# Windowed attention before two feed-forward parts: first blocks of 128 columns, tables and sums in pieces, the general pass placed last

## Chip, cores and metric

The kernel runs on one core of a Trainium2 chip. The metric is the device time of one execution in microseconds; lower is better. All operands are float32.

## The reference, cut to what matters

```python
scores = q @ k.T / sqrt(D)                       # B=2, H=8, S=768, D=64
rel = pos[:, None] - pos[None, :]
keep = (pos[None, :] < n_global) | ((rel >= 0) & (rel < n_local))   # 8 and 96
scores = where(keep, scores - slope[h] * dist, -1e9)                # dist: |rel|, or n_local for global keys
x = softmax(scores) @ v                          # then (B*S, H*D) = (1536, 512)
...
for e in range(4):                               # gated part, F = 1024
    out += p[:, e:e+1] * (relu(x @ w1[e]) @ w2[e])
h = out @ w_in                                   # last part, F = 2048
y = (h * clip(h + 3, 0, 6) / 6) @ w_out
```

## The kernel before, in words

**Attention.** A *pair* is two heads on a chunk of 256 queries: 6 chunks (three for each of two batches) by 4 pairs of heads, 24 pairs. A pair has two blocks of 128 queries. Each block sees 256 columns of keys: 96 previous and 32 first ones, then its own 128. The first block of a batch has nothing before it, so its first 128 columns are masked by a table of its own. For every pair (`plan_pair`, L305) the steps are: load of q and k into one of four places of `qkraw` (L316) and of v (L323) on SP's queue; scores on PE (L344); bias by table, scale and minimum on DVE (L357); exponential and row sum on ACT (L371); reciprocal on DVE (L380, L381); normalisation on POOL (L389); transposes on PE (L402); copies out of PSUM on ACT for the first block and on DVE for the second (L414); products with v on PE (L426); copy of the result on ACT (L436). The tables (`plan_bias`, L271) are made on DVE for head 0 (L279 to L282, L285) and scaled on POOL for heads 1 to 7, twice seven instructions of 256 columns (L298).

**Feed-forward parts.** 48 steps of 256 hidden columns each. Every float32 operand is split into a high part (ACT cast, L230) and a low part (DVE subtraction, L235), and a product is three matmuls (L858, L862, L865 for the first layer, L1037, L1040, L1041 for the second). The first layer is computed by seven products with sums of blocks, in the manner of Strassen and Winograd: four sums of x (T1 to T4 in `plan_x`, L576; on POOL for batch 0, L614) and four sums of weights (S1 to S4 in `plan_weights`, L713; on POOL for the first two steps, L781 to L784, else on DVE). `finish` (L1066) copies a finished output out of PSUM, four blocks of 512 + 256 columns; the 256-column parts of two blocks share a bank. For the last part it issues the stores of the output (L1093).

**Order.** Nothing is ordered by hand. `Plan` (L53) holds pieces (engine, cost, emit, what they come after, rank) and lists them: whenever an engine is free in the plan's own time it takes the ready piece of lowest rank. The result is a fixed order for each engine. In gaps of PE's plan before the first feed-forward product, `keep_warm` (L240) puts matmuls on zeros.

**Two passes.** The device reads `n_global` and `n_local`, computes a flag (L160 to L167) and loads it into a register of every engine (L175). `body(True)` is the pass above, `body(False)` a general one for other sizes:

```python
    with tc.If(is_fast == 1) as cmp:
        body(True)
    with cmp.Else():
        body(False)
```

## Time and profile before

| | |
|---|---|
| median of 3 runs | 866.78 us (866.5 to 867.9) |
| the profiled execution | 867.49 us, its span 865.6 us |
| PE busy | 848.6 us (98%), granted clock 0.992 on the mean |
| DVE, ACT, POOL busy | 664.4, 406.1, 71.1 us |
| DMA | 148.14 MB, 171 GB/s on the mean |

The span runs from the first to the last instruction; the 1.9 us beside it are start and end of the execution. Busy time is time in which an engine has an instruction at work. Matmuls are pipelined, so a busy PE may still run at half its clock or wait inside; the stretches must be read one by one. POOL works only in the first 107 us.

### The profile page before, as it was taken

The page shows a single profiled execution, that of the slowest core. Times are in us where ns is not written, and L with a number is a line of the kernel's source. Part 1 is how long each engine was busy: PE and PEld are TensorE (multiplying, and loading weights), DVE is VectorE, ACT ScalarE, POOL GpSimd, SP SyncE. Part 2 cuts the span into 40 slices and gives each one's busy share as a digit, 9 for nine tenths or more (in the row PEclk, how much of TensorE's full clock was granted, in tenths as well). Part 3 has the DMA queues.
Part 4 walks back from the last instruction along what each step waited for, and adds up shares of the span by engine and source line. Part 5 has one row for each costly group of instructions (what it writes and reads, how often), then busy time and mean ns, then how long its engine had stood idle before and what let it go on. Part 6 is the DMA issues. An engine that isn't in the chain of part 4 may idle for free.

```text
span 865.6 us, 13712 instructions
## 1 busy us (share of the span) xinstructions
PE 848.6 (98%) x5117; PEld 770.7 (89%) x5117; DVE 664.4 (77%) x1362; ACT 406.1 (47%) x846; POOL 71.1 (8%) x127
## 2 busy tenths in 40 slices
PE   8998999999999999999999999999999999999996
PEld 6675799999999999999999999999999999999996
DVE  5889889898989988798786878878888774645442
ACT  5897853443434333443333333234655454545441
POOL 5478700000000000000000000000000000000000
PEclk9997999999999999999999999999999999999999
DMA  7663545455564666536656566556344353733402
GB/s 247 222 204 110 198 170 166 167 186 158 188 214 154 225 194 193 202 122 205 208 174 207 180 202 212 161 163 227 107 160 169 135 184 120 243 122 115 152 1 77
DMA packets 55833, 148.14 MB, mean 171 GB/s; under 512 B 6352, under 2 KB 6480, under 8 KB 55760
## 3 DMA queue, kind: packets, MB, share of 16 engines
q1 hardware_dynamic: 55472, 146.51, 51.6%
q8 instruction: 42, 0.69, 0.3%
q10 hardware_dynamic: 288, 0.69, 0.2%
q14 instruction: 31, 0.25, 0.1%
HBM read 110.45 MB, written 36.72 MB: 170 GB/s over the span
## 4 chain that ended last, share of the span: by engine, by line
PE 92%; DVE 3%; DMA 2%; ACT 1%; POOL 1%; issue 1%; DVEq 0%; SPq 0%; POOLq 0%
PE o L1040 15%; PE o L1041 15%; PE o L1037 15%; PE x_x L858 8%; PE x_x L865 8%; PE x_x L862 8%; PE w_w L862 6%; PE w_w L858 6%; PE w_w L865 6%; PE att_q L402 2%; PE att_q L426 2%; PE att_q L344 2%; DMA w<-qkraw 1%; DVE xol L235 1%; DMA wr<-in_w 1%
## 5 line engine op out<-in xcount | busy, mean ns | idle before, releaser
L1040 PE MATMUL o<-hh,w2l 128*128 128x512 f32 (+1 forms) x768 | 259.4, 338 | 0.0
L1041 PE MATMUL o<-hl,w2h 128*128 128x512 f32 (+1 forms) x768 | 258.9, 337 | 0.0
L1037 PE MATMUL o<-hh,w2h 128*128 128x512 f32 (+1 forms) x768 | 257.8, 336 | 0.0
L882 ACT COPY snap<-x_x 128x384 f32<-128x384 f32 x144 | 69.0, 479 | 199.2 <-PE x_x L865 199.2
L895 DVE TENSOR_TENSOR c_c<-w_w,snap 128x384 f32<-128x384 f32 x144 | 80.0, 555 | 105.1 <-ACT w2h L230 61.0
L1041 PEld LDWEIGHTS o<-hl,w2h 128*128 128x128 f32 x768 | 144.4, 188 | 16.0
L1037 PEld LDWEIGHTS o<-hh,w2h 128*128 128x128 f32 x768 | 144.4, 188 | 13.3
L1040 PEld LDWEIGHTS o<-hh,w2l 128*128 128x128 f32 x768 | 144.5, 188 | 12.6
L858 PE MATMUL x_x<-xoh,w1h 128*128 128x384 f32 x384 | 129.3, 337 | 0.0
L865 PE MATMUL x_x<-xoh,w1l 128*128 128x384 f32 x384 | 129.1, 336 | 0.0
L862 PE MATMUL x_x<-xol,w1h 128*128 128x384 f32 x384 | 128.9, 336 | 0.0
L862 PE MATMUL w_w<-xol,w1h 128*128 128x384 f32 x288 | 97.2, 338 | 1.2 <-DVE xol L235 1.2
L858 PE MATMUL w_w<-xoh,w1h 128*128 128x384 f32 x288 | 96.9, 336 | 0.3 <-DVE c_c L895 0.3
L865 PE MATMUL w_w<-xoh,w1l 128*128 128x384 f32 x288 | 96.8, 336 | 0.0
L230 ACT CAST w2h<-wr 128x1024 fp32r<-128x1024 f32 x48 | 50.4, 1050 | 65.2 <-PE o L1041 63.6
L858 PEld LDWEIGHTS x_x<-xoh,w1h 128*128 128x128 f32 x384 | 72.3, 188 | 2.5 <-ACT xf L436 0.3
L862 PEld LDWEIGHTS x_x<-xol,w1h 128*128 128x128 f32 x384 | 72.3, 188 | 2.1 <-DVE xol L235 0.2
L964 ACT CAST hh<-c_c 128x384 fp32r<-128x384 f32 x96 | 49.4, 515 | 51.7 <-DVE c_c L933 51.4
L865 PEld LDWEIGHTS x_x<-xoh,w1l 128*128 128x128 f32 x384 | 72.0, 188 | 0.0
L230 ACT CAST w1h<-wr 128x512 fp32r<-128x512 f32 x96 | 46.7, 510 | 49.4 <-PE w_w L862 47.4
L235 DVE TENSOR_TENSOR w2l<-wr,w2h 128x1024 fp32r<-128x1024 f32 x48 | 58.4, 1217 | 0.7 <-ACT w2h L230 0.7
L862 PEld LDWEIGHTS w_w<-xol,w1h 128*128 128x128 f32 x288 | 54.0, 188 | 3.7 <-DVE xol L235 1.5
(87 smaller groups left out, 1166.2 us busy)
## 6 DMA issues: line engine op xcount, KB each, us to landing
wr<-in_w SPq DMA_DIRECT2D x64, 512.0 KB, 4.2
wr<-w SPq DMA_DIRECT2D x32, 512.0 KB, 3.7
kept<-w1h SPq DMA_DIRECT2D x24, 512.0 KB, 2.9
kept<-w1l SPq DMA_DIRECT2D x24, 512.0 KB, 4.9
w1h<-kept SPq DMA_DIRECT2D x24, 512.0 KB, 3.9
w1l<-kept SPq DMA_DIRECT2D x24, 512.0 KB, 5.2
qkraw<-in_w_in SPq DMA_DIRECT2D x16, 512.0 KB, 4.4
qkraw<-in_w_out SPq DMA_DIRECT2D x16, 512.0 KB, 4.3
```

Source lines behind the costliest of these rows:

```text
L230: nc.scalar.copy(out_ap, src)
L235: nc.vector.tensor_tensor(out_ap, src, hi_ap.bitcast(F32), op=ALU.subtract)
L344: nc.tensor.matmul(m["s", qb, j][:, 0 : 2 * P], raw[rows, qb * P : (qb + 1) * P], raw[rows, w0 : w0 + 2 * P], start=True, stop=True,)
L858: nc.tensor.matmul(ps_, wh[:, a, cols], xh[:, o, kc, :], start=start and kc == 0, stop=False, skip_group_check=True,)
L862: nc.tensor.matmul(ps_, wh[:, a, cols], xl[:, o, kc, :], start=False, stop=False, skip_group_check=True)
L865: nc.tensor.matmul(ps_, wl[:, a, cols], xh[:, o, kc, :], start=False, stop=last, skip_group_check=True)
L882: nc.scalar.copy(m["n", n][:], m["x"][:, :HT])
L895: nc.vector.tensor_tensor(m[name][:], m["w"][:, :HT], m["n", n][:], op=ALU.add)
L964: nc.scalar.copy(at(0), room_for())
L1037: nc.tensor.matmul(o, wh, hh, start=first and own and f == 0, stop=False, skip_group_check=True)
L1040: nc.tensor.matmul(o, wl, hh, start=False, stop=False, skip_group_check=True)
L1041: nc.tensor.matmul(o, wh, hl, start=False, stop=end, skip_group_check=True)
```

## The change

- `Plan` knows a port: pieces on POOL, and DVE pieces marked `port=True`, are not planned to overlap each other. Idle time for `keep_warm` is now counted from the end of the engine's last piece.
- `body(True)` is no longer in a condition. The flag is computed and read after it, and the general pass follows under `is_fast == 0`.
- The order of pairs is by batch, then heads, then chunk (before: chunk, then heads). A pair of heads needs its tables only when its turn comes, and their ranks say so.
- In the first block of a batch, scores, bias, exponentials, normalisation, transposes, copy and products use 128 columns instead of 256. The tables are 128 columns for that block and 256 for others (before 256 each), and the constants are half as wide. The load of the second pair moves from ACT's queue to SP's.
- Sums of x are made in two halves of 384 columns, with ranks that rise piece by piece; sums of weights are four pieces instead of one. The weights of the first two steps are planned ahead of the sums of x.
- In `finish` the 256-column part of a block is copied when its own products are done (before: with its neighbour's), and each store of the output is split into 512 and 256 columns.

The diff, cut to its core:

```diff
+        if port or engine == "pool":
+            self.ported.add(len(self.pieces) - 1)
...
+                for place, (rank, i) in enumerate(now[engine]):
+                    if i not in self.ported or port <= free[engine]:
+                        start = free[engine]
+                        break
+                else:
+                    events = [port] * bool(now[engine]) + [t for t, _ in later[engine][:1]]
+                    place, start = None, min(events, default=None)
...
+                self.idle(engine, start - ended.get(engine, 0.0))
             emit()
-            free[engine] = start + cost
+            free[engine] = ended[engine] = start + cost
...
-            pairs = [(c, hp) for c in range(NCH) for hp in range(NHP)]
+            pairs = [(b * CPB + c, hp) for b in range(B) for hp in range(NHP) for c in range(CPB)]
...
+            rel, gidx = fast_c[:, : 2 * P], fast_c[:, 2 * P :]
+            window, first = tabs[:, 0, P:], tabs[:, 0, :P]
+
+            def base():
+                nc.vector.tensor_scalar(out=window, in0=rel, scalar1=nl, scalar2=NONE, op0=ALU.is_ge, op1=ALU.mult)
+                nc.vector.scalar_tensor_tensor(out=window, in0=rel, scalar=-4.0, in1=window, op0=ALU.mult, op1=ALU.add)
+                nc.vector.tensor_scalar(out=gidx, in0=gidx, scalar1=ng, scalar2=NONE, op0=ALU.is_ge, op1=ALU.mult)
+                nc.vector.scalar_tensor_tensor(
+                    out=first, in0=gidx, scalar=nl4, in1=window[:, P:], op0=ALU.add, op1=ALU.max
+                )
+                keys = window[:, NPREV:P]
+                nc.vector.scalar_tensor_tensor(
+                    out=keys, in0=gidx[:, :NG], scalar=nl4, in1=keys, op0=ALU.add, op1=ALU.max
+                )
+
+            made = plan.add("dve", 1.7, base, [started["fast_c"]], -2.0, port=True)
...
+                        "pool", 0.46 if kind else 0.3, scaled, [made], (h // 2 * CPB - 2) * CH + 0.1 * h + 0.5 * kind
+                    )
...
+                first = slice(P * (1 - kind), 2 * P)
...
+                            m["s", qb, j][:, used], raw[rows, qb * P : (qb + 1) * P],
+                            raw[rows, w0 : w0 + 2 * P][:, used], start=True, stop=True,
...
+                h0 = 1 if c % CPB == 0 and qb == 0 else 0
+                halves.append(range(h0, 2))
+                used = slice(h0 * P, 2 * P)
+                normal = []
+                for j in range(2):
+
+                    def normalise(qb=qb, j=j, used=used):
                         nc.gpsimd.tensor_scalar(
-                            out=m["t"][:, qb, j, :], in0=m["t"][:, qb, j, :], scalar1=m["sm"][:, qb, j : j + 1],
+                            out=m["t"][:, qb, j, used], in0=m["t"][:, qb, j, used], scalar1=m["sm"][:, qb, j : j + 1],
                             scalar2=1.0, op0=ALU.mult, op1=ALU.mult,
                         )
 
-                f = plan.add("pool", 0.96, normalise, [r], rank)
+                    normal.append(plan.add("pool", 0.32 if h0 else 0.48, normalise, [r], rank))
...
+                        for h in range(h0, 2):
...
+                    for h in halves[qb]:
...
+                    def emit(j):
+                        if which not in made:
+                            room_for()
+                        adders[adder].tensor_tensor(
+                            made[which][:, j, :], left()[:, j, :], right()[:, j, :], op=ALU.subtract
+                        )
+
+                    e = []
+                    cost = t_dve(HT) if adder == "dve" else t_tt(HT)
+                    for j in range(2):
+                        e.append(
+                            plan.add(adder, cost, lambda j=j: emit(j), waits + wait + extra, next(rank), port=True)
...
+                    summed = loaded
+                    for n in range(4):
+                        summed = plan.add(
+                            adder, cost, lambda n=n: sums(n), [summed] + wait_s, rank, port=True
...
-                    other = ends[2 * (d - d % 2) + 3]
                     lot = ((d, 0, ends[2 * d], slice(0, 512), slice(0, 512)),
-                           (4 + d // 2, 1, other, slice(d % 2 * 256, d % 2 * 256 + 256), slice(512, S)))
-                    got = []
+                           (4 + d // 2, 1, ends[2 * d + 1], slice(d % 2 * 256, d % 2 * 256 + 256), slice(512, S)))
...
+                            def leave(a=a, d=d, toks=toks):
+                                nc.sync.dma_start(out[d, :, b * S : (b + 1) * S][:, toks], a[:, toks])
+
+                            plan.add("load", 0.8, leave, [e], -9.0)
...
+            for i in range(2):
+                plan_weights(i)
+            x_done[0, False] = plan_x(0, x_ready[0], steps_from(26.0, 0.8), "pool")
...
-    with tc.If(is_fast == 1) as cmp:
-        body(True)
-    with cmp.Else():
+
+    body(True)
+    flag = const.tile([P, 2], I32, name="flag")
+    nc.vector.tensor_scalar(out=nv[:, 4:5], in0=nl, scalar1=1.0, scalar2=None, op0=ALU.is_ge)
+    nc.vector.scalar_tensor_tensor(
+        out=nv[:, 5:6], in0=nl, scalar=float(NPREV + 1), in1=nv[:, 4:5], op0=ALU.is_le, op1=ALU.mult
+    )
+    nc.vector.scalar_tensor_tensor(
+        out=flag[:, 0:1], in0=ng, scalar=float(NG), in1=nv[:, 5:6], op0=ALU.is_le, op1=ALU.mult
+    )
+    is_fast = nc.values_load(flag[0:1, 0:1], min_val=0, max_val=1)
+    with tc.If(is_fast == 0):
         body(False)
 
 ```

Where the order moves, three places. First POOL at the start (`L298` is now `L304`, `L389` now `L403`; a name such as `t_0_244` is the tile of one pair). Before:

```order
L175 TENSOR_LOAD flag
L1132 COMPARE_AND_BRANCH
L298 ISA
L298 TENSOR_SCALAR tabs<-tabs 128x256 x14
L389 TENSOR_SCALAR t_0_244<-t_0_244,sm_0_262 128x256 x4
L389 TENSOR_SCALAR t_1_270<-t_1_270,sm_1_287 128x256 x4
```

and now:

```order
L304 ISA
L304 TENSOR_SCALAR tabs<-tabs 128x128
L304 TENSOR_SCALAR tabs<-tabs 128x256
L304 TENSOR_SCALAR tabs<-tabs 128x128 x2
L304 TENSOR_SCALAR tabs<-tabs 128x256 x2
L304 TENSOR_SCALAR tabs<-tabs 128x128 x2
L304 TENSOR_SCALAR tabs<-tabs 128x256 x2
L304 TENSOR_SCALAR tabs<-tabs 128x128 x2
L304 TENSOR_SCALAR tabs<-tabs 128x256
L403 TENSOR_SCALAR t_0_217<-t_0_217,sm_0_227 128x128 x2
L403 TENSOR_SCALAR t_0_217<-t_0_217,sm_0_227 128x256 x2
```

The read of the flag and the branch are gone from here, and thirteen table instructions, seven of them of 128 columns, stand ahead of the first pair's normalisation; the fourteenth follows the second pair's.

Second POOL where batch 0 ends (`L614` is now `L640`; in `t_3_1_826` the chunk is 3 and the pair of heads 1; t3, t4, t6, t5 are T1, T2, T4, T3). Before:

```order
L389 TENSOR_SCALAR t_3_1_826<-t_3_1_826,sm_3_1_842 128x256 x2
L614 TENSOR_TENSOR t3_0_3086_914<-xf_0_145 128x768
L614 TENSOR_TENSOR t4_0_3086_941<-xf_0_145,t3_0_3086_914 128x768
L389 TENSOR_SCALAR t_3_1_826<-t_3_1_826,sm_3_1_842 128x256 x2
L614 TENSOR_TENSOR t6_0_3086_970<-xf_0_145,t4_0_3086_941 128x768
L614 TENSOR_TENSOR t5_0_3086_993<-xf_0_145 128x768
L389 TENSOR_SCALAR t_3_2_871<-t_3_2_871,sm_3_2_887 128x256 x4
L389 TENSOR_SCALAR t_3_3_916<-t_3_3_916,sm_3_3_983 128x256 x4
L781 TENSOR_TENSOR wsum_0_1055<-wr1_0_329 128x256
L782 TENSOR_TENSOR wsum_0_1055<-wr1_0_329 128x256
L783 TENSOR_TENSOR wsum_0_1055<-wsum_0_1055,wr1_0_329 128x256
L784 TENSOR_TENSOR wsum_0_1055<-wr1_0_329,wsum_0_1055 128x256
```

and now:

```order
L403 TENSOR_SCALAR t_4_0_804<-t_4_0_804,sm_4_0_836 128x256 x4
L640 TENSOR_TENSOR t3_0_3229_915<-xf_0_125 128x384 x2
L640 TENSOR_TENSOR t4_0_3229_953<-xf_0_125,t3_0_3229_915 128x384
L403 TENSOR_SCALAR t_5_0_853<-t_5_0_853,sm_5_0_873 128x256 x4
L403 TENSOR_SCALAR t_3_1_895<-t_3_1_895,sm_3_1_947 128x128 x2
L403 TENSOR_SCALAR t_3_1_895<-t_3_1_895,sm_3_1_947 128x256 x2
L403 TENSOR_SCALAR t_4_1_949<-t_4_1_949,sm_4_1_980 128x256 x4
L640 TENSOR_TENSOR t4_0_3229_953<-xf_0_125,t3_0_3229_915 128x384
L640 TENSOR_TENSOR t6_0_3229_1096<-xf_0_125,t4_0_3229_953 128x384 x2
L403 TENSOR_SCALAR t_5_1_1030<-t_5_1_1030,sm_5_1_1052 128x256 x4
```

Three halves now stand together, then the normalisations of pairs 14, 15 and 16 (counted from 0 in the new order), then three more halves; T3's two follow pair 19. The sums of weights are no longer here; they stand in batch 0, between the normalisations of pairs 3 to 11. On PE the product of S2 and T2 stands ahead of the transposes of pair 17 (`t_5_1`), and ten products instead of eight stand ahead of attention's last products with v.

Third DVE at the very end (`L1083` is now `L1120`; o_1, o_3 are PSUM tiles of 512 columns, o_4 and o_5 the shared ones). Before:

```order
L952 SCALAR_TENSOR_TENSOR qkraw<-qkraw,c_c_8458 128x384
L972 SCALAR_TENSOR_TENSOR hl_8410<-qkraw,hh_8409 128x384 x2
L1083 COPY xf_146<-o_1_7603 128x512
L1083 COPY xf_146<-o_4_7594 128x256 x2
L1083 COPY xf_146<-o_3_7673 128x512
L1083 COPY xf_146<-o_5_7654 128x256 x2
L1132 UNCONDITIONAL_BRANCH
```

and now:

```order
L1011 SCALAR_TENSOR_TENSOR hl_8377<-qkraw,hh_8376 128x384 x2
L1120 COPY xf_126<-o_4_7561 128x256
L1120 COPY xf_126<-o_1_7570 128x512
L1120 COPY xf_126<-o_4_7561 128x256
L1120 COPY xf_126<-o_5_7621 128x256
L1120 COPY xf_126<-o_3_7640 128x512
L1120 COPY xf_126<-o_5_7621 128x256
L1184 TENSOR_LOAD flag
```

The 256-column copies of blocks 0 and 2 have moved ahead of the 512-column copies of blocks 1 and 3, and the read of the flag follows the last copy (on SP it stands near the start, behind the first ten loads; the instructions that compute the flag stand on DVE between those of the tables).

## Rows read from the trace of the kernel before

**Rows 1.** Busy time of each engine by stretch, with records, granted clock and DMA share

```profile
core 0: us, PE busy (x) PEld busy (x) DVE busy (x) ACT busy (x) POOL busy (x), PEclk, DMA share, GB/s
0.00:15.19 15.19, 11.71 (x57) 8.86 (x57) 8.64 (x44) 6.28 (x21) 6.77 (x21) 1.00 0.65 218
15.19:58.40 43.21, 41.85 (x390) 29.88 (x390) 34.01 (x146) 37.18 (x127) 24.07 (x51) 1.00 0.74 237
58.40:80.00 21.60, 16.59 (x109) 10.87 (x108) 19.71 (x42) 15.01 (x40) 19.06 (x20) 0.76 0.28 81
80.00:111.70 31.70, 31.36 (x294) 24.63 (x293) 27.16 (x90) 26.97 (x81) 21.21 (x37) 1.00 0.59 188
111.70:859.10 747.40, 747.09 (x4274) 696.49 (x4272) 574.07 (x1040) 320.64 (x581) 0.00 (x0) 1.00 0.51 169
```

**Rows 2.** Chain of waits, 44 to 52 us: start us, us, what

```profile
46.01 1.06 PE att_q L344 x8
47.07 1.02 PE att_q L426 x16
48.10 1.02 PE att_q L402 x8
```

**Rows 3.** Order of time, chain of waits and DMA issues, first 17 us

```profile
7.02 2.08 PE L344 MATMUL att_q<-qkraw 64*128 64x256 f32 x8 [2.27 <-DVE flag L165]
8.32 6.36 POOL L298 TENSOR_SCALAR tabs<-tabs 128x256 f32<-128x256 f32 x14 [7.32 <-DVE tabs L282]
...
14.66 3.67 POOL L389 TENSOR_SCALAR t<-t,sm 128x256 f32<-128x256 f32 x8
...
15.19 0.44 PE att_q L402 x2
...
qkraw<-in_fast SPq DMA_DIRECT2D x1, 384.0 KB, 5.8
```

**Rows 4.** Groups of instructions by line and shape, 0 to 111.8 us

```profile
L414 ACT COPY at<-att_q 128x512 f32<-128x512 f32 x24 | 14.1, 586 | 3.7 <-PE att_q L402 3.7
L436 ACT COPY xf<-att_q 128x256 f32<-128x256 f32 x23 | 8.6, 373 | 5.3 <-DVE mn L357 4.8 <-PE att_q L426 0.4
L230 ACT CAST w2h<-wr 128x1024 fp32r<-128x1024 f32 x2 | 2.1, 1039 | 1.4 <-DMA wr<-in_w 1.4
```

**Rows 5.** Order of time on POOL, 58 to 78 us

```profile
58.48 0.94 POOL L389 TENSOR_SCALAR t<-t,sm 128x256 f32<-128x256 f32 x2 [1.26 <-ACT xf L436]
59.38 1.83 POOL L614 TENSOR_TENSOR t<-xf 128x768 f32<-128x768 f32 x1
61.30 2.43 POOL L614 TENSOR_TENSOR t<-xf,t 128x768 f32<-128x768 f32 x1
63.71 3.11 POOL L389 TENSOR_SCALAR t<-t,sm 128x256 f32<-128x256 f32 x2
...
72.71 4.90 POOL L389 TENSOR_SCALAR t<-t,sm 128x256 f32<-128x256 f32 x8 [0.88 <-DVE sm L381]
```

**Rows 6.** Order of time on DVE and ACT, 59 to 73 us; a wait on ACT

```profile
59.93 5.48 DVE L235 TENSOR_TENSOR xol<-xf,xoh 128x768 fp32r<-128x768 f32 x3
61.01 0.38 ACT L436 COPY xf<-att_q 128x256 f32<-128x256 f32 x1
...
71.71 0.37 ACT L436 COPY xf<-att_q 128x256 f32<-128x256 f32 x1
72.46 0.93 DVE L235 TENSOR_TENSOR xol<-t,xoh 128x768 fp32r<-128x768 f32 x1
...
ACT w2h L230 <- DMA wr<-in_w: 1.4, 1, 1.4
```

**Rows 7.** Order of time and DMA issues at the end

```profile
858.39 1.46 DVE L1083 COPY xf<-o 128x512 f32<-128x512 f32 x3 [2.73 <-PE o L1041]
859.59 0.81 SPq L1093 DMA_DIRECT2D out_t<-xf  x2
...
out_t<-xf SPq DMA_DIRECT2D x4, 384.0 KB, 3.1
```

More of the change, by code (lines that the diff above doesn't have):

```diff
@@ L65, in __init__, with add @@
         self.pieces = []
+        self.ported = set()
         self.idle = idle
-    def add(self, engine, cost, emit, after=(), rank=0.0):
+    def add(self, engine, cost, emit, after=(), rank=0.0, port=False):
         self.pieces.append((engine, cost, emit, after, rank))
+        if port or engine == "pool":
+            self.ported.add(len(self.pieces) - 1)
         return len(self.pieces) - 1
@@ L94, in emit @@
                 heappush(later[self.pieces[i][0]], (0.0, i))
-        for _ in range(n):
+        count = 0
+        while count < n:
             best = None
@@ L284, in first @@
-            def first():
-                nc.vector.memset(tabs[:, 0, 0:P], NONE)
-                part(slice(0, P))
-            base = [
-                plan.add("dve", 1.1, first, [started["fast_c"]], -2.0),
-                plan.add("dve", 1.4, lambda: part(slice(P, 3 * P)), [started["fast_c"]], -1.5),
-            ]
-            for kind in range(2):
-                started[0, kind] = base[kind]
-                for h in range(1, H):
+            rel, gidx = fast_c[:, : 2 * P], fast_c[:, 2 * P :]
@@ L296, in scaled @@
+            made = plan.add("dve", 1.7, base, [started["fast_c"]], -2.0, port=True)
+            for h in range(H):
+                for kind in range(2):
+                    if h == 0:
+                        started[h, kind] = made
+                        continue
                     def scaled(h=h, kind=kind):
-                        cols = slice(kind * 2 * P, (kind + 1) * 2 * P)
+                        cols = slice(P, 3 * P) if kind else slice(0, P)
                         nc.gpsimd.tensor_scalar(
@@ L336, in plan_pair, with scores @@
                     s_users.append(su)
-                def scores(qb=qb, tags=tags, w0=w0):
+                def scores(qb=qb, tags=tags, w0=w0, used=first):
                     for j in range(2):
@@ L344, in scores, with bias @@
                         nc.tensor.matmul(
-                            m["s", qb, j][:, 0 : 2 * P], raw[rows, qb * P : (qb + 1) * P],
-                            raw[rows, w0 : w0 + 2 * P], start=True, stop=True,
+                            m["s", qb, j][:, used], raw[rows, qb * P : (qb + 1) * P],
+                            raw[rows, w0 : w0 + 2 * P][:, used], start=True, stop=True,
                         )
-                s_in = plan.add("pe", 0.64, scores, [loaded] + waits, rank)
+                s_in = plan.add("pe", 0.64 if kind else 0.34, scores, [loaded] + waits, rank)
                 readers.append(s_in)
-                def bias(qb=qb, kind=kind):
+                def bias(qb=qb, kind=kind, used=first):
                     if "t" not in m:
@@ L363, in plan_pair, with exponentials @@
                 after = [s_in, started[2 * hp, kind], started[2 * hp + 1, kind]]
-                e = plan.add("dve", 0.8, bias, after + wait_t, rank)
+                e = plan.add("dve", 0.75 if kind else 0.5, bias, after + wait_t, rank)
                 for su in s_users:
                     su.append(e)
-                def exponentials(j, qb=qb):
+                def exponentials(j, qb=qb, used=first):
                     if "sm" not in m:
@@ L423, in values @@
                 for qb in range(CH):
-                    for h in range(2):
+                    for h in halves[qb]:
                         for j in range(2):
@@ L427, in values @@
                                 m["o"][j * D : (j + 1) * D, qb * P : (qb + 1) * P], m["v"][:, h, qb, j, :],
-                                m["at", qb][:, j, h, :], start=h == 0, stop=h == 1,
+                                m["at", qb][:, j, h, :], start=h == halves[qb][0], stop=h == 1,
                             )
-            v = plan.add("pe", 1.05, values, [e for e, _ in copied] + [v_in] + wait_o, rank)
+            v = plan.add("pe", 1.05 if len(halves[0]) == 2 else 0.8, values, [e for e, _ in copied] + [v_in] + wait_o, rank)
             v_users.append(v)
@@ L692, in plan_convert @@
                 for j, step in enumerate((begin, join, exponent, guard, power, scale_low)):
-                    last = plan.add("dve", costs[j], step, [last] + (waits if j == 0 else []), rank)
+                    last = plan.add("dve", costs[j], step, [last] + (waits if j == 0 else []), rank, port=True)
                     r_users.append(last)
```

184 lines of the change are left out of this document (84 added, 100 removed).

## Prediction, made before the changed kernel ran

> **What bounds the kernel now.** I read the busy time by stretch first, then the chain of waits, then the instructions in order of time around the places where the stretches differ. The stretches [rows 1] show two kernels in one. From 111.70 to 859.10 us (the feed-forward part alone) PE is busy 747.09 of 747.40 us at granted clock 1.00: 4274 matmul records at 747.40/4274 = 0.175 us each, no idle to win. Before 111.70, with attention, PE is not the bound everywhere. The reader is to see there the third stretch, 58.40 to 80.00: PE is busy 16.59 of 21.60 us, for only 109 records, at a granted clock of 0.76, while DVE is busy 19.71 and POOL 19.06.
>
> Work against time there: in the smooth part of the chain a pair of heads costs PE 1.06 + 1.02 + 1.02 = 3.10 us (scores, values, transposes; 8, 16 and 8 records) [rows 2], so 32 records a pair, on the mean 0.097 us a record. 15.19 to 58.40: 390 records x 0.097 = 37.8 us of work in 43.2, lost 5.4. 58.40 to 80.00: the feed-forward part has two products in it, 12 records (2.1 us); the other 97 make 9.4; lost 21.6 - 11.5 = 10.1. 80.00 to 111.70: 36 records of six products (6.3) and 258 of attention (25.0); lost 0.4. Before 15.19, from the first scores at 7.02 [rows 3], 28 records of scores (3.7 us) in 8.2; lost 4.5. So some 20 us in all, half of them in one stretch.
>
> **The change part by part.** The sum is made against the profiled execution, 867.49 us (span 865.6); the median of the runs shown is 866.78, 0.7 below it.
>
> *Start.* Before, PE's first scores wait for the flag until 7.02, POOL begins 14 table instructions at 8.32 and ends them 6.36 us later, and only then (14.66) normalises the first pair, whose transposes start at 15.19 [rows 3]. Now nothing waits for the flag; the constants' load is half as long (384 KB, which took 5.8 us to land), and POOL does 13 table instructions ahead of the first normalisation, seven of 128 columns. With 6.36/14 = 0.45 us for 256 columns and about 0.27 for 128 (an estimate: between half and all of it) that is 6 x 0.45 + 7 x 0.27 = 4.6 instead of 6.4 us, minus 1.8; the tables' own base starts a little earlier but all of it is now in front of POOL. I take -2.2; the bounds are -1.0 (128 columns cost nearly as much as 256, the load gains nothing) and -3.0 (the base is 1 us earlier as well).
>
> *128 columns in first blocks.* Eight of 24 pairs begin a batch. In each PE saves half of two scores matmuls (1.06/4 = 0.265), two of eight transposes (0.255) and four of sixteen records of values (0.255): 0.775, in all 6.2 us [rows 2]. ACT copies 512 columns in 586 ns and 256 in 373 [rows 4], 0.107 per 128, so two exponentials and a copy save 0.21 + 0.21 = 0.43 a pair, 3.4 in all. Which of the two counts? In batch 1 PE has feed-forward products to fill every gap (31.36 of 31.70 busy [rows 1]), so PE's price: 4 x 0.775 = 3.1. In batch 0 PE is not the bound (5.4 lost) and ACT, busy 37.18 of 43.21, is nearer: 4 x 0.43 = 1.7. I take -4.8; bounds -3.4 and -6.2.
>
> *Sums in pieces, and their place.* The first two of POOL's four sums of 768 columns take 1.83 and 2.43 us, and all four stand in front of normalisations: after two at 58.48 only two more run until a whole set starts at 72.71 [rows 5]. A DVE row of the same time shows the collision: three subtractions ran 5.48 us, where one takes 0.93 elsewhere, and two POOL normalisations took 3.11 instead of 2 x 0.46 [rows 5, 6]. The result copies of pairs 12 and 13 (counted from 0; the first two of batch 1) stand at 61.01 and 71.71 [rows 6]; PE's own pace is 3.1 [rows 2]. Now three halves (about 1.0 us each, estimated from 1.83 for the whole) precede pair 14's normalisation, the other five come after pairs 16 and 19, and the sums of weights, which stood behind them, are made during batch 0. Attention would so be delayed by about 3 us at a time instead of 10. But the same work must still go through DVE, POOL and ACT, whose load stays near PE's: I let 4.5 of the 10.1 us stay, so -5.6; bounds 0 and -10.1.
>
> *Work pulled forward.* Before, ACT casts 512 + 256 + 1024 + 1024 columns of weights in batch 0, at 1.04 us per 1024 [rows 4] 2.9 us, and once waits 1.4 for a load [rows 6]; in the new order these are 4608 columns, 4.7 us, and POOL adds eight weight sums. Where ACT is nearest to the bound this costs: +1.0, bounds -1.4 (the wait for the load goes) and +2.9 (it comes twice).
>
> *A new wait.* In the final copies the 256-column half of an even block leaves without waiting for its neighbour. Both halves are in one bank, and PE's next 256-column group now waits for that copy; everything on PE is queued behind it. It has six 512-column matmuls of slack (at least 6 x 0.175 = 1.05 us) against a copy of about 0.4 us (three, one of them of 512 columns, take 1.46 [rows 7]) and DVE's queue ahead of it. Eight such waits, two in each of four endings: +0.5, bounds 0 and +3.
>
> *The end.* Before, DVE's last three copies take 1.46 from 858.39, and the last two output stores of 384 KB are issued together from 859.59, 3.1 us to landing [rows 7]. Now block 2 has left before, and after the last copy only 256 columns remain: one copy of 0.4 fewer, and half the bytes: -0.9. The register load and jump that stood at the start now follow the last work on each engine; SP reads the flag near its start, so I hide them behind the last output store. If they do not hide, they cost what the start loses by them, about 0.8. Bounds -0.1 and -1.5.
>
> Shorter weight sums on DVE after attention, another order of ties: nothing, since PE's stretch is full for 747 us; if that cover were gone each would cost its extra start, some tenths.
>
> Sum: -2.2 - 4.8 - 5.6 + 1.0 + 0.5 - 0.9 = -12.0, so 855.5 against 867.49, and 854.8 against the median: **855**.
>
> **The rivals.** *A, the stretch keeps its loss.* The pieces collide as the wholes did: DVE and POOL were busy 19.7 and 19.1 of 21.6 us there [rows 1], so work spread out is still the same work. Then -5.6 is 0: -6.4, 861. Against it: part of these busy times is waiting for each other (5.48 for 2.8). The Trainium skill, page "SBUF — State Buffer", section "SBUF: two separate sides", says that DVE and GpSimd take a shared pair of ports as an exclusive lock, held for a whole instruction, so that the loser stands still. The trace agrees in kind [rows 5, 6]; by that rule alone short pieces shorten the longest stop and leave the sum of the two engines' work, and the time would be A's.
>
> *B, PE stays full.* With ties broken well PE waits for nothing after the first transposes: -3.0 - 6.2 - 10.1 - 1.5 = -20.8, 847. For it: 80.00 to 111.70 shows attention and products together with 0.4 us lost. Against: ACT has to cast more there than before.
>
> *C, slower.* The second half of the second sum now stands behind the normalisations of three pairs on POOL. The product that reads it stands on PE ahead of pair 17's transposes. If its cast (ACT) and its low part (DVE) come late, PE stops with all of attention behind it, and the clock drops as it did here (0.76). The other terms give -6.4, so this decides from the point where the stretch loses 10.1 + 6.4 = 16.5 us; at 19 it gives 870.
>
> *D, it does not do what it says:* instructions of 128 columns cost as much as of 256. Then -4.8 is 0 and the start gives -1.0: -6.0, 861. Against it: the transposes' and copies' rows scale with columns.
>
> **How the numbers follow.** Forecast (850 to 858): 0.55. A: 0.17. B: 0.14. C, slower by more than 0.2% (about what a measurement of this kernel can tell from no change, 1.7 us): 0.06. D: 0.04. Within 0.2%, if A comes with the worst ends of the other terms: 0.04. So faster 0.55 + 0.17 + 0.14 + 0.04 = 0.90, same 0.04, slower 0.06. The range takes in B's 847 and A's and D's 861 with a little of the unknown waits: 847 to 862.
>
> **What would show it.** Start right: first transposes near 13.0 instead of 15.19. First blocks right: about 0.775 us of PE less in each of eight pairs, values in 12 records. Sums right: the results of pairs 12 and 13 are 5 us apart instead of 10.7, clock near 1.00 there. Attention should end near 99 to 101 us with ten products done instead of eight, then 0.175 a record again. The end right: about 5.6 us from PE's last matmul. It is wrong if a stretch of ten us with PE at 70% is still there (A), if PE waits for copies of its own output in the four endings, or if the tail grows.

## Result and profile after the change

The changed kernel takes **857.76 us** (median of 4 runs, 856.07 to 858.09) against 867.28 of the kernel before beside it: ratio 0.9887, 95% interval 0.987 to 0.9904, so 9.8 us faster (8.3 to 11.3). Forecast were 855.0, range 847 to 862. The profiled execution is 857.74, 9.75 less than the 867.49 of before; forecast were 12.0 less.

Busy time by stretch, kernel after; the columns are those of [rows 1], the cuts lie at like events (first transposes, twelfth result, a result copy behind the sums, end of attention, PE's last matmul). The third stretch ends with the fifteenth result before and with the sixteenth now:

```profile
core 0: us, PE busy (x) PEld busy (x) DVE busy (x) ACT busy (x) POOL busy (x), PEclk, DMA share, GB/s
0.00:12.84 12.84, 8.90 (x60) 7.12 (x60) 6.83 (x41) 6.30 (x22) 5.25 (x20) 1.00 0.75 251
12.84:55.45 42.61, 41.40 (x364) 28.96 (x364) 35.75 (x147) 36.83 (x127) 32.01 (x60) 0.96 0.81 256
55.45:71.59 16.14, 15.19 (x134) 11.43 (x134) 14.95 (x52) 15.29 (x45) 14.38 (x21) 1.00 0.76 265
71.59:101.70 30.11, 29.14 (x260) 23.16 (x257) 27.14 (x83) 24.54 (x76) 18.99 (x32) 1.00 0.30 90
101.70:847.36 745.66, 745.15 (x4262) 694.21 (x4260) 573.79 (x1049) 320.08 (x577) 0.00 (x0) 1.00 0.52 169
847.36:856.00 8.64, 0.00 (x0) 0.00 (x0) 0.44 (x2) 0.00 (x0) 0.00 (x0) 0.68 0.17 57
```

PE's last matmul ends at 847.36 instead of 859.06 (859.10 is the cut of [rows 1]): **11.7 us earlier**. The rest of the program, 6.5 us before, is 8.6: **2.1 us longer**. So all of the shortfall against the forecast, and a little more, is in the last row. The stretch in which PE was busy 16.59 of 21.60 us at clock 0.76 [rows 1] is gone: from 55.45 to 71.59 PE is busy 15.19 of 16.14 at clock 1.00. From the twelfth result copy to the fifteenth it is 12.97 us now (55.45 to 68.42) and was 21.95. Attention ends at 101.7 with ten products done (4262 records follow, 0.175 us each as before); before, 111.7 and eight. The two copies of the kernel before, in order of time on ACT:

```profile
58.06 0.37 ACT L436 COPY xf<-att_q 128x256 f32<-128x256 f32 x1 [0.29 <-DVE mn L357]
...
80.01 0.37 ACT L436 COPY xf<-att_q 128x256 f32<-128x256 f32 x1
```

The first microseconds, in order of time on POOL and PE, kernel after (they answer to [rows 3]):

```profile
7.52 4.79 POOL L304 TENSOR_SCALAR tabs<-tabs 128x128 f32<-128x128 f32 x13 [6.52 <-DVE tabs L287]
12.41 3.46 POOL L403 TENSOR_SCALAR t<-t,sm 128x128 f32<-128x128 f32 x8
...
12.84 0.69 PE L416 MATMUL att_q<-qkraw,t 128*128 128x128 f32 x2 [1.12 <-POOL t L403]
```

Thirteen tables take 4.79 us instead of fourteen 6.36, and the first transposes come at 12.84 instead of 15.19. The sums' stretch on POOL, and the result copies of pairs 11 to 14 on ACT, kernel after (for [rows 5, 6]):

```profile
57.72 2.69 POOL L640 TENSOR_TENSOR t<-xf 128x384 f32<-128x384 f32 x2
60.38 1.00 POOL L640 TENSOR_TENSOR t<-xf,t 128x384 f32<-128x384 f32 x1
61.35 7.11 POOL L403 TENSOR_SCALAR t<-t,sm 128x256 f32<-128x256 f32 x12
...
55.45 0.37 ACT L457 COPY xf<-att_q 128x256 f32<-128x256 f32 x1
58.01 0.37 ACT L457 COPY xf<-att_q 128x256 f32<-128x256 f32 x1 [0.21 <-DVE mn L366]
62.28 0.37 ACT L457 COPY xf<-att_q 128x256 f32<-128x256 f32 x1 [0.52 <-DVE mn L366]
68.42 0.38 ACT L457 COPY xf<-att_q 128x256 f32<-128x256 f32 x1
```

After three halves of the sums, twelve normalisations run in one go; before, two of them ran behind two whole sums and took 3.11, and a whole set only from 72.71 on [rows 5]. Pairs 12 and 13 are now 4.3 us apart instead of 10.7.

The end, kernel after (for [rows 7]). DVE's last copies in order of time:

```profile
846.68 1.14 DVE L1120 COPY xf<-o 128x512 f32<-128x512 f32 x2 [0.96 <-PE o L1080]
```

SP's instructions at the jump (L1185) and at the program's close (L1254), in the view by line: count, duration in ns (least, median, most), first and last start:

```profile
L1185 SPq COMPARE_BRANCH  x1: 53/53/53, 848.3 to 848.3; - x1
L1185 SPq EVENT_SEMAPHORE  x8: 17/17/17, 851.5 to 854.1; - x8
L1254 SPq EVENT_SEMAPHORE  x10: 17/28/28, 854.2 to 855.9; - x10
```

The waits of SP's queue in the last 9 us, and of PE from 101.7 us on (us in total, times, longest):

```profile
SPq L1185 <- SPq L1185: 5.3, 2, 3.2
...
PE w_w L897 <- DVE c_c L934: 0.5, 1, 0.5
```

The last copy ends at 847.82. SP issues the last store, jumps over the general pass at 848.3, and stands still twice, 3.2 us and then 2.1 (5.3 in two waits, on nothing but itself), before the closing work begins at 854.2. The kernel before jumped there too, over Else, with one stop (same view by line):

```profile
L1132 SPq COMPARE_BRANCH  x1: 46/46/46, 860.4 to 860.4; - x1
L1208 SPq EVENT_SEMAPHORE  x10: 17/28/28, 864.2 to 865.5; - x10
```

The Trainium skill, page "Runtime: NRT & Kernel Launch", section "Instruction fetch mechanics", says that a taken branch whose target is not yet loaded forces a fetch of instructions before the engine can go on. The trace agrees in kind (the jump itself is 53 ns, the stop behind it 3.2 us); the page gives no duration. The DMA view of the changed kernel counts loads of instructions as a kind of their own: four packets from 848.3 to 851.5 and two from 851.5 to 854.1, and no packet of a store in the second stop, so the output has landed before it begins; in the kernel without the general pass (below) it is one packet from the last copy to the end. The view does not say for which engine a packet is. Nor is the first stop only SP's wait for its stores: DVE, which issues none, stands still behind the same jump from 848.0 to 851.7. PE's row speaks for the other new wait: 0.5 us in all of the feed-forward part, and nowhere for the final copies.

### The profile page after: what moved, and what is told of

Read it like the earlier page. It is cut to its first block, busy times and chain, and to the rows that moved or that the text cites. A ratio compares the mean times of both kernels' runs of the same rounds, so it can differ in the third digit from the quotient of the medians.

```text
span 856.0 us, 13645 instructions
## 1 busy us (share of the span) xinstructions
PE 839.8 (98%) x5071; PEld 764.9 (89%) x5071; DVE 658.9 (77%) x1370; ACT 403.0 (47%) x846; POOL 70.6 (8%) x131
## 4 chain that ended last, share of the span: by engine, by line
PE 91%; ACT 3%; DMA 3%; DVE 1%; POOL 0%; issue 0%; SPq 0%; DVEq 0%
PE o L1079 15%; PE o L1080 15%; PE o L1076 15%; PE x_x L897 8%; PE x_x L904 8%; PE x_x L901 8%; PE w_w L897 6%; PE w_w L901 6%; PE w_w L904 6%; ACT t L380 2%; PE att_q L447 2%; PE att_q L416 1%; DMA wr<-in_w 1%; PE att_q L353 1%; DMA w<-qkraw 1%; DMA qkraw<-in_fast 1%
## 5 line engine op out<-in xcount | busy, mean ns | idle before, releaser
L1080 PE MATMUL o<-hl,w2h 128*128 128x512 f32 (+1 forms) x768 | 259.0, 337 | 0.0
L934 DVE TENSOR_TENSOR c_c<-w_w,snap 128x384 f32<-128x384 f32 x144 | 80.0, 556 | 103.4 <-ACT w2h L234 59.0
L1080 PEld LDWEIGHTS o<-hl,w2h 128*128 128x128 f32 x768 | 144.4, 188 | 16.0
L897 PE MATMUL x_x<-xoh,w1h 128*128 128x384 f32 x384 | 129.4, 337 | 0.0
L897 PE MATMUL w_w<-xoh,w1h 128*128 128x384 f32 x288 | 97.2, 338 | 0.5 <-DVE c_c L934 0.5
L234 ACT CAST w2h<-wr 128x1024 fp32r<-128x1024 f32 x48 | 50.4, 1050 | 64.8 <-PE o L1080 61.6
L897 PEld LDWEIGHTS x_x<-xoh,w1h 128*128 128x128 f32 x384 | 72.3, 188 | 3.0 <-issue 1.0
L234 ACT CAST w1h<-wr 128x512 fp32r<-128x512 f32 x96 | 46.4, 510 | 49.1 <-PE w_w L901 45.2
L239 DVE TENSOR_TENSOR w2l<-wr,w2h 128x1024 fp32r<-128x1024 f32 x48 | 58.7, 1222 | 1.6 <-ACT w2h L234 1.6
L897 PEld LDWEIGHTS w_w<-xoh,w1h 128*128 128x128 f32 x288 | 54.1, 188 | 4.0 <-DVE c_c L934 1.3
```

The source lines that it names most:

```text
L234: nc.scalar.copy(out_ap, src)
L239: nc.vector.tensor_tensor(out_ap, src, hi_ap.bitcast(F32), op=ALU.subtract)
L897: nc.tensor.matmul(ps_, wh[:, a, cols], xh[:, o, kc, :], start=start and kc == 0, stop=False, skip_group_check=True,)
L934: nc.vector.tensor_tensor(m[name][:], m["w"][:, :HT], m["n", n][:], op=ALU.add)
L1080: nc.tensor.matmul(o, wh, hl, start=False, stop=end, skip_group_check=True)
```

## Experiments

Twelve kernels, each with four to six executions. A difference to the changed kernel is worked out from the two ratios to the kernel before (each measured beside its own runs of it) times 867.4 us, with the two half-intervals added in quadrature. The differences all share the one ratio of the changed kernel, from four executions, so an error in it moves all of them the same way.

**The end.** *The general pass left out:*

```diff
 body(True)
-flag = const.tile([P, 2], I32, name="flag")
...
-with tc.If(is_fast == 0):
-    body(False)
```

> The changed kernel without the flag, the jump and the general pass behind it (which is left out). In the changed kernel the last copy ends at 847.81 and the program at 856.0: 8.2 us, in which SP jumps (848.26), resumes at 851.54, handles eight semaphores until 854.15, and only then ends the program. Theory J (the jump over the general pass sets the end): the end is then the landing of the last store (1.7 to 2.9 us after its issue at 847.85) and about 1.7 us of closing work, so 3 to 4 us less, near 854. Rival S (the stores themselves set it): within 0.7 us of the changed kernel, 857.8.

852.98 us, ratio 0.9844 (0.9827 to 0.9861): 3.7 +- 2.1 us less. Last copy 846.53, end 850.2: 3.7 us instead of 8.2. Theory J holds in size: the jump and what hangs on it are 4.5 us of the end in these two profiles.

*The last batch's stores issued by ACT:*

```diff
-nc.sync.dma_start(out[d, :, b * S : (b + 1) * S][:, toks], a[:, toks])
+nc.scalar.dma_start(out[d, :, b * S : (b + 1) * S][:, toks], a[:, toks])
...
-plan.add("load", 0.8, leave, [e], -9.0)
+plan.add("act", 0.05, leave, [e], -9.0)
```

> The last batch's eight output stores are issued by ACT instead of SP; the general pass stays. Theory J: SP, which has no other work late, jumps and handles its eight semaphores before the last copy; what is left behind the last copy is the jump of DVE and ACT (DVE's took 848.02 to 851.70) and the closing 1.7 us: 2 to 3 us less, near 855. If instead the same eight semaphores have to wait on ACT, or a store issued by ACT lands later (rival S), nothing is won: 857 to 858.

**854.12 us**, ratio 0.9842 (0.9829 to 0.9856): 3.9 +- 1.9 us less than the changed kernel, with everything computed. It is the version that beats both. Of the 3.9, 2.6 stand in the end of the two profiles (5.6 against 8.2 us from last copy to end; the last copies themselves end 0.2 us apart). The rest is not shown to be the stores' doing: the granted clock over the whole execution is 0.997 to 0.999 in its five runs and 0.994 to 0.997 in the four of the changed kernel. SP's and ACT's instructions at the jump, this kernel:

```profile
L1185 SPq EVENT_SEMAPHORE  x8: 17/17/17, 846.6 to 851.0; - x8
L1185 SPq COMPARE_BRANCH  x1: 53/53/53, 806.2 to 806.2; - x1
L1185 ACTq COMPARE_BRANCH  x1: 54/54/54, 849.7 to 849.7; - x1
L1185 ACTq EVENT_SEMAPHORE  x1: 17/17/17, 852.3 to 852.3; - x1
```

SP now jumps at 806.2, 40 us ahead of its next instruction, so that a stop there costs nothing; what is left at the end is ACT's, 849.7 to 852.3. From the last copy (848.02) to the end (853.6) 5.6 us.

*The condition ahead of the fast pass, with Else, as before:*

```diff
+is_fast = nc.values_load(flag[0:1, 0:1], min_val=0, max_val=1)
...
+with tc.If(is_fast == 1) as cmp:
+    body(True)
+with cmp.Else():
+    body(False)
```

> The changed kernel with the condition where it stood before: flag and jump ahead of the fast pass, the general pass behind Else. Theory J: from the last copy to the end 5.8 us as in the kernel before instead of 8.2 (-2.4), and the start later by the flag and the jump, about 1.0 (PE's first scores at 5.64 in the changed kernel, 7.02 in the kernel before): 856.4, between 855.5 and 857. Rival F (the wait for the flag was most of the start's 2.35 us): 857.8 or more.

856.85 us, ratio 0.9874 (0.9857 to 0.9892): 1.1 +- 2.1 less, not told apart from nothing. The forecast time came out, its reason did not: the first transposes come at 14.29, 1.45 later, but the end is 7.3 us (last copy 847.19, end 854.5), not 5.8. So where the condition stands is at most a small part (8.2 - 7.3 = 0.9) of what made the end longer.

*The final copies and stores as before:*

```diff
-(4 + d // 2, 1, ends[2 * d + 1], slice(...), slice(512, S))
+(4 + d // 2, 1, other, slice(...), slice(512, S))
...
-nc.sync.dma_start(out[d, :, b * S : (b + 1) * S][:, toks], a[:, toks])
+nc.sync.dma_start(out[d, :, b * S : (b + 1) * S], a)
```

> The changed kernel with the final copies as before: the 256-column half of an even block waits for its neighbour, and each output block leaves in one store of 384 KB. My forecast gave the new wait of PE +0.5 (0 to 3) and the earlier, smaller stores -0.9. If both terms hold: 858.2. In the changed kernel's trace PE waits nowhere for these copies, and SP's jump sets the end whatever the store's size; by that reading only the third copy of 0.41 us in front of the last store counts: 858.2 as well, with the last store issued 0.4 later, and no PE wait gained or lost. Slower than 859 or faster than 857 would speak against both.

855.5 us, ratio 0.9856 (0.984 to 0.9871): 2.7 +- 2.0 less. That is what I had written would speak against both readings, and it does: the new finish costs, though its stores are smaller and leave sooner. In the profiles 1.6 of the 2.7 stand in the end (6.6 against 8.2). The profiled execution, 858.01, is the slowest of the four and shows no gain in all: PE waits 2.0 us in all for DVE steps of the feed-forward part (tile c_c; 0.5 in the changed kernel), and its last copy ends at 849.62. SP's jump and what follows, this kernel:

```profile
L1184 SPq COMPARE_BRANCH  x1: 53/53/53, 850.2 to 850.2; - x1
L1184 SPq EVENT_SEMAPHORE  x8: 17/17/17, 854.0 to 854.5; - x8
L1253 SPq EVENT_SEMAPHORE  x10: 17/28/28, 854.6 to 856.2; - x10
```

With four stores SP stands still once (850.3 to 854.0), does the same eight semaphores in 0.5 us and goes on into the closing work; with eight stores it stops a second time. That holds in all nine traces with eight stores from SP ahead of a jump, for 1.2 to 2.4 us, but not at one place: among the eight semaphores in three of them, behind them in five (with whole sums, below, they run from 865.3 to 865.9 and the closing work begins at 867.6), and from 851.2 to 853.2 with the condition first. The end of all kernels, each from one profile:

| kernel | condition | stores of the last batch | last copy | end | between |
|---|---|---|---|---|---|
| before | first, Else | 4, SP | 859.85 | 865.6 | 5.8 |
| condition first | first, Else | 8, SP | 847.19 | 854.5 | 7.3 |
| old final copies | last | 4, SP | 849.62 | 856.2 | 6.6 |
| changed | last | 8, SP | 847.82 | 856.0 | 8.2 |
| stores from ACT | last | 8, ACT | 848.02 | 853.6 | 5.6 |
| no general pass | none | 8, SP | 846.53 | 850.2 | 3.7 |

Seven more kernels below have the changed kernel's end and take 7.1 to 8.7 us for it, so 8.2 against 7.3 proves nothing, while 5.8 and 6.6 lie below all nine with eight stores from SP behind a jump. Shown is: against 3.7 without a jump, the jump costs 3.4 to 5.0 us in these nine, and the new finish with its eight stores some 1.5 more than the old one. The copies were undone together with the stores, so the run does not separate them. Why SP stops a second time is open; in the changed kernel it does not wait for the output, which has landed by then.

**The stretch of the sums.** *Whole sums at one rank, weight sums in one piece:*

```diff
-for j in range(2):
-    e.append(plan.add(adder, cost, lambda j=j: emit(j), waits + wait + extra, next(rank), port=True))
+e.append(plan.add(adder, cost, emit, waits + wait + extra, next(rank), port=True))
...
-plan_x(0, x_ready[0], steps_from(26.0, 0.8), "pool")
+plan_x(0, x_ready[0], repeat(25.0), "pool")
```

> The changed kernel (857.8), with POOL's four sums of 768 columns whole again, at one rank as before, and its weight sums in one piece of four instructions; the weights still come ahead of them in the plan. Theory P (the pieces heal the stretch after the first batch, my forecast's 5.6 us): near 863.4. Rival O (it is healed because the weight sums now run during the first batch, whatever the size of the pieces): within 2 us of 857.8.

871.08 us, ratio 1.0038 (1.0024 to 1.0053): **13.1 +- 2.0 us more**, slower than the kernel before. POOL, DVE and the result copies of pairs 12 and 13 on ACT in order of time, this kernel:

```profile
61.96 1.82 POOL L639 TENSOR_TENSOR t<-xf 128x768 f32<-128x768 f32 x1
63.85 2.44 POOL L639 TENSOR_TENSOR t<-xf,t 128x768 f32<-128x768 f32 x1
68.99 1.82 POOL L639 TENSOR_TENSOR t<-xf,t 128x768 f32<-128x768 f32 x1 [2.70 <-DVE xol L239]
70.79 0.78 POOL L403 TENSOR_SCALAR t<-t,sm 128x256 f32<-128x256 f32 x1
74.45 1.93 POOL L639 TENSOR_TENSOR t<-xf 128x768 f32<-128x768 f32 x1 [2.88 <-DVE xol L239]
76.36 5.27 POOL L403 TENSOR_SCALAR t<-t,sm 128x256 f32<-128x256 f32 x9
...
62.56 5.41 DVE L239 TENSOR_TENSOR xol<-xf,xoh 128x768 fp32r<-128x768 f32 x3
...
63.63 0.38 ACT L457 COPY xf<-att_q 128x256 f32<-128x256 f32 x1 [0.15 <-PE att_q L447]
84.07 0.37 ACT L457 COPY xf<-att_q 128x256 f32<-128x256 f32 x1 [0.79 <-DVE mn L366]
```

and its busy times from 70 to 80 us (columns of [rows 1]):

```profile
70.00:80.00 10.00, 6.51 (x21) 4.55 (x20) 9.72 (x20) 3.34 (x6) 7.12 (x9) 0.50 0.00 0
```

It is the mechanism of the kernel before [rows 5, 6], only longer: one normalisation between 62 and 76 us, because the third and fourth sum wait for DVE's low parts (2.70 and 2.88), which ran 5.41 us beside the first two; PE has 21 records in ten us, at clock 0.50. Pairs 12 and 13 are 20.4 us apart.

*Weights planned behind the sums again:*

```diff
-for i in range(2):
-    plan_weights(i)
 x_done[0, False] = plan_x(0, x_ready[0], steps_from(26.0, 0.8), "pool")
```

> The changed kernel with the weights of the first two steps planned behind the sums again, as before; the sums stay in pieces. Theory P: the stretch stays healed, and the term for work pulled forward (+1.0, bounds -1.4 and +2.9) goes: 856 to 859, most likely 856.8. Rival O: the weight sums stand behind the sums again and hold up what follows: 861 or more, with results of pairs 12 to 14 some 5 us later than in the changed kernel.

862.91 us, ratio 0.9948 (0.9935 to 0.996): 5.3 +- 1.9 more. Neither reading was right as a whole. The time is rival O's, but pairs 12 to 14 come only 2 to 3 us later than in the changed kernel (1.5 of it are there before the sums). The last result comes at 106.0 instead of 101.8: the rest is lost behind, where the weight sums now stand between normalisations (order of time on POOL, this kernel):

```profile
82.70 1.41 POOL L820 TENSOR_TENSOR wsum<-wr 128x256 f32<-128x256 f32 x2 [0.94 <-DVE xol L239]
...
85.57 4.28 POOL L403 TENSOR_SCALAR t<-t,sm 128x256 f32<-128x256 f32 x7
```

*Both of these edits together:*

> The changed kernel with whole sums at one rank (+13.3 us alone, 871.1) and with the weights of the first two steps planned behind them (+5.1 alone, 862.9): as in the kernel before in both, and the rest of the change kept. If the two add up (theory A): 876. If whole sums cost that much only where the weights stand ahead of them (theory I, they compete for DVE and POOL in one stretch), the stretch should lose about what it lost before, 5.6 to 10 us more than the changed kernel: 863 to 868.

872.77 us, ratio 1.006 (1.0046 to 1.0074): 15.0 +- 1.9 more. Theory A falls too, by little: by the ratios the two alone add up to 18.4, and 15.0 is 3.4 +- 2.5 below that; theory I's 863 to 868 is out. Whole sums cost 9.7 with the weights behind them and 13.1 with the weights ahead; weights behind cost 5.3 with pieces and 1.9 with whole sums.

*Without the plan's rule on POOL and DVE:*

```diff
-if port or engine == "pool":
-    self.ported.add(len(self.pieces) - 1)
```

> The changed kernel without the plan's new rule that a piece on POOL and a marked piece on DVE are never planned for the same time. My forecast gave the rule no term. Theory N (it only shuffles pieces that find room anyway): within 1.5 us of 857.8. Rival L (POOL and DVE hold each other up, as in the stretch of before, and the rule keeps them apart): 2.5 us slower or more, with longer POOL normalisations (over 2.3 us for four, against 1.85) in the trace.

862.18 us, ratio 0.9939 (0.9922 to 0.9956): 4.5 +- 2.1 more, rival L. Four normalisations take up to 2.82 us where 1.85 is the undisturbed time (order of time on POOL, this kernel):

```profile
70.18 2.65 POOL L401 TENSOR_SCALAR t<-t,sm 128x256 f32<-128x256 f32 x4 [1.49 <-DVE sm L388]
...
77.02 2.82 POOL L401 TENSOR_SCALAR t<-t,sm 128x256 f32<-128x256 f32 x4 [0.67 <-DVE sm L388]
```

Such stretched rows are in the changed kernel too (7.11 us for twelve), so the run shows what the rule's order is worth, not that every us of it is contention.

What heals the stretch itself can be read from the result copies. From the twelfth to the fifteenth it is 12.97 us in the changed kernel, 13.2 without the rule, 14.3 with the weights behind the sums, 24.0 with whole sums and the weights behind them, and 27.0 with whole sums alone; 21.95 before. So the pieces, with their ranks, heal it; the weights' place is worth about 1 us there and the rule next to nothing. What these two bring lies elsewhere in the plan: without the rule the twelfth result already comes 2.2 us later.

**First blocks, order, tables.** *256 columns in first blocks* (with the bias of the other blocks, so the mask of the first ones is left out):

```diff
-first = slice(P * (1 - kind), 2 * P)
+first = slice(0, 2 * P)
...
-h0 = 1 if c % CPB == 0 and qb == 0 else 0
+h0 = 0
```

> The first blocks of a batch take 256 columns again in scores, bias, exponential, normalisation, transposes, copies and values; their bias comes from the window's table, so the outputs of those blocks differ. All else as in the changed kernel. My forecast for this part was 4.8 us (3.4 where ACT's price counts everywhere, 6.2 where PE's counts everywhere): 862.6, between 861 and 864. If 128 columns cost as much as 256: no difference. If ACT, busy 88 to 100 percent from 25 to 55 us, holds batch 0 and PE batch 1: 1.7 plus 3.1, the same 862.6.

860.62 us, ratio 0.9922 (0.9907 to 0.9936): 3.0 +- 1.9 more. Below the forecast 4.8 and below its lower bound 3.4, but 4.8 is inside the interval. The rival that 128 columns are worth nothing is out.

*The old order of pairs:*

```diff
-pairs = [(b * CPB + c, hp) for b in range(B) for hp in range(NHP) for c in range(CPB)]
+pairs = [(c, hp) for c in range(NCH) for hp in range(NHP)]
```

> The changed kernel with the pairs in the old order, all four pairs of heads of a chunk before the next chunk, instead of three chunks of a pair of heads. My forecast gave the order no term. Theory N: the thirteen tables run ahead of the first normalisation in the changed kernel all the same, so the order is worth nothing: within 1.5 us of 857.8. Rival T (the order spreads tables and the short first blocks): 2 us slower or more, pairs 1 to 3 waiting for tables.

857.93 us, ratio 0.9896 (0.988 to 0.9912): 0.8 +- 2.0 more. No difference that can be measured.

*Tables held back until they are needed* (heads 2 to 7, each group behind a normalisation):

```diff
-"pool", 0.46 if kind else 0.3, scaled, [made], ...
+"pool", 0.46 if kind else 0.3, scaled, [made, held[h // 2]], ...
```

> The bias tables of heads 2 to 7 wait, in the plan, for the normalisation of pairs 0, 2 and 5, so that POOL makes two tables ahead of the first normalisation instead of thirteen. Theory T (in the changed kernel POOL's thirteen tables, 7.52 to 12.31, still hold up the first pair, whose sums are ready at 10.52, and the wait costs PE its clock: 0.76 from 12.8 to 20): first transposes near 11.0, no fall of the clock, 2 to 3.5 us less. Rival A (ACT is the bound of the first batch, 36.8 of 42.6 us busy, so PE's lost time there was hidden anyway, and the tables come back between normalisations): between 0.5 less and 1 more.

863.94 us, ratio 0.9959 (0.9945 to 0.9973): 6.2 +- 1.9 more; theory T falls, and rival A allowed only 1. The first transposes come at 12.53, not 11.0: POOL makes two tables and then waits 3.36 us for DVE's sums, which stand in DVE's queue behind the biases of the next pairs. What is lost is lost elsewhere, since the whole plan moved. Waits of ACT and PE from 39 to 51 us, this kernel (us in total, times, longest):

```profile
ACT w1h L234 <- DMA wr<-in_w: 2.3, 1, 2.3
...
PE att_q L453 <- DVE mn L369: 3.1, 1, 3.1
```

ACT reaches a weight cast before its load has landed, and everything on ACT stands behind it. The changed kernel meets the same load 0.55 us late.

*Only heads 4 to 7 held back, with the stores from ACT:*

> Stores of the last batch from ACT (854.1 alone), and only the tables of heads 4 to 7 held until the first pair is normalised: six tables ahead of it instead of thirteen, about 2.2 us instead of 4.8, which is when the first pair's sums are ready. Theory T: first transposes near 11.0, 1 to 2 us less than 854.1: 852 to 853. Rival Q (the held tables alone changed the planned order, and that order meets late loads, as where all were held: 6 us slower): 856 or more.

854.75 us, ratio 0.9861 (0.9838 to 0.9884), against 854.12 with the stores alone: nothing gained. The first transposes stay at 12.83 although the tables are done at 9.4: again DVE's queue, not POOL's, is what the first pair waits for. Theory T is out a second time.

## Why the prediction was right, and where it was not

**Up to PE's last matmul the sum was right, in part by luck:** -2.2 - 4.8 - 5.6 + 1.0 + 0.5 = -11.1 forecast, -11.7 measured.

*Start.* -2.2 forecast, first transposes 2.35 earlier: right at that point, and the condition alone is 1.45 of it. How much of it arrives is not shown: in this profile PE had idled 1.12 us there, and its clock is 0.76 from 12.84 to 20.00. With the condition first, where the transposes come 1.45 later and the clock stays at 1.00, the twelfth result comes at 55.34 against 55.45 here.

*First blocks.* -4.8 forecast, 3.0 +- 1.9 by undoing. Right in kind, perhaps too large: ACT is busy 36.83 of 42.61 us in the first batch.

*Sums in pieces.* -5.6, with 4.5 of 10.1 us left to be lost. At the prices of [rows 2], counted by kind, PE's work from 55.45 to 71.59 is 13.7 of 16.1 us: 2.4 lost. The step was right in mechanism and too small in size. Undoing it costs 13.1, more than the 10.1 that were to be had, since whole sums fit this plan worse than the old one (27.0 us from the twelfth to the fifteenth result against 21.95). Rivals A and C did not come: no long stop, neither there nor ahead of pair 17.

*Work pulled forward.* +1.0 (-1.4 to +2.9): **the step that failed in sign**. I priced the casts on ACT in batch 0, and the price is not to be seen: with the weights behind the sums again the twelfth result comes 1.5 us later, not earlier. What the move brings at the sums I had put into the -5.6 without a size of its own, and what it brings behind them I had not seen; moved back, the weights cost 5.3 us in all. In the same way I gave the plan's rule on POOL and DVE no term at all; it is worth 4.5. That the front came out right is luck to that extent: the sums' term was lowered from 10.1 to 5.6 by judgement, and not each part was sized. The parts also do not add: 13.1, 5.3, 4.5 and 3.0 are more than the 11.7 that all brought, as each was taken out of a plan that had been made with the others.

The Trainium skill, page "SBUF — State Buffer", section "SBUF: two separate sides", on which rival A rested, is borne out in kind by the stretched normalisations (2.82 us against 1.85). Rival A's 861 did not come, with 857.76 measured; 862.18, where the pieces stay and only the rule goes, comes near it in time, but the stretch of the sums stays healed there (13.2 us).

*The new wait.* +0.5; PE waits nowhere for a final copy: 0, the lower bound.

*The end.* -0.9 (-0.1 to -1.5): **wrong, it is +2.1**, and these 3.0 us are more than the whole gap between the 855.5 forecast for the profiled execution and its 857.74. The step that failed is "I hide them behind the last output store". I had priced the store's bytes (384 KB, 3.1 us [rows 7]) and taken its landing for the end. But SP issues the last store and jumps behind it, and its stop of 3.2 us and the second of 2.1 outlast the landing; bytes were not the price, SP's instructions were. The kernel before paid 3.8 us for a jump of its own at 860.4, which was in its trace, unread; so the jump is no new cost at the end, and half the bytes could win nothing. Of the 2.4 us by which the end from the last copy grew (5.8 to 8.2), the old finish takes back 1.6 and the old place of the condition 0.9, each by one profile.

## What to carry to other kernels

The end of a program is a chain of its own: read the queue that issues the last store to its very last instruction, and look for jumps there; moving the last stores to an engine with little left to do gave 3.9 us here, 2.6 of them seen in the end, about what 128 columns in the first blocks gave (3.0). In a planned order a long piece costs what stands behind it in its queue: whole sums ahead of normalisations cost 13.1 us. Parts undone one at a time do not add up. Holding work back until it is needed is no gain if another in-order queue is what the consumer waits for.

## What the runs showed of the hardware that was not expected

A jump stops its engine for microseconds: SP 3.2 us in the changed kernel and 3.8 in the kernel before, though the instruction itself takes 0.05; in the changed kernel DVE stands still 3.7 us, ACT 2.8 and POOL 1.5 behind theirs, and on PE it shows as one instruction of 3.96 us.

PE's clock falls at places that the order of work does not explain. Without the general pass the same instructions run up to there, but the first scores take 1.65 us instead of 0.93, PE idles 0.23 us instead of 1.12 ahead of the first transposes, and the clock stays. PE in order of time, changed kernel and then the one without the general pass:

```profile
5.64 0.93 PE L353 MATMUL att_q<-qkraw 64*128 64x128 f32 x8 [1.24 <-DMA qkraw<-in_qk]
```

```profile
5.62 1.65 PE L353 MATMUL att_q<-qkraw 64*128 64x128 f32 x8 [0.87 <-DMA qkraw<-in_qk]
...
12.84 0.68 PE L416 MATMUL att_q<-qkraw,t 128*128 128x128 f32 x2 [0.23 <-POOL t L403]
```

The stretch behind, in the same two kernels (columns of [rows 1]):

```profile
12.84:20.00 7.16, 7.14 (x44) 4.84 (x46) 4.04 (x17) 4.41 (x16) 5.25 (x12) 0.76 0.39 118
```

```profile
12.84:20.00 7.16, 7.12 (x61) 4.68 (x62) 4.74 (x22) 5.55 (x21) 5.67 (x14) 1.00 0.52 146
```

In 7.16 us that is 61 records instead of 44; at the mean 0.097 us of a record, 1.6 us. In the changed kernel the clock fell after PE had stood idle three times (1.24, 0.53 and 1.12 us). But idle time alone does not decide it: with the stores from ACT PE stands idle 0.94, 0.53 and 1.09 us at the same places, the first scores take 0.93 us too, and the clock stays at 1.00 until 25 us. What decides, and why the same scores took 0.93 or 1.65, is open. Nor does this fall alone set the front: with the old final copies the clock stays at 1.00 through all of attention, yet DVE waits 1.0 us there for the load of the gate's inputs (gate<-in_dpt), a wait that the changed kernel does not have, and the last result comes at 101.67 against 101.77. Without the general pass neither came, and it is 100.20. Both chances, a fall of the clock and a late load, lie within the 1 to 2 us by which runs of one kernel differ here.
